# Fewer, longer VectorE instructions in a cached-attention decode kernel, and one small weight load in six pieces

## The chip, the cores and the metric
One core of a Trainium2 chip. The metric is the device time of one execution of the whole program in microseconds (us). The engines are TensorE (PE, its weight loads PEld), VectorE (DVE), ScalarE (ACT), GpSimd (POOL) and SyncE (SP, which here only issues transfers); 16 DMA engines move the data.

## What is computed
Four attention layers follow each other on one token's vector x of 640 numbers. Layers 0 and 2 use the caches and weights A, layers 1 and 3 those of B, so each cache is read twice. Each layer has 32 heads of 192 numbers and a cache of 8192 positions.

```python
q = (x @ wq).reshape(B, Sq, H, Dh)...
scores = jnp.einsum("bhqd,bhkd->bhqk", q, k_cache) * (Dh ** -0.5)
p = _softmax(scores, axis=-1)
o = jnp.einsum("bhqk,bhkd->bhqd", p, v_cache)
return ... @ wo

x = x + _A_ref(_layernorm(x, axis=-1), A_k_cache, A_v_cache, A_wq, A_wo)
x = x + _B_ref(_layernorm(x, axis=-1), B_k_cache, B_v_cache, B_wq, B_wo)
x = x + _A_ref(_layernorm(x, axis=-1), A_k_cache, A_v_cache, A_wq, A_wo)
x = x + _B_ref(_layernorm(x, axis=-1), B_k_cache, B_v_cache, B_wq, B_wo)
```

All is bf16 in memory, with float32 sums.

## The kernel before
The work goes by pairs of heads, 16 pairs in a layer, in the order of `ORDER` (layer 3 runs nearly backward). A pair's K is 6.3 MB, and so is its V: partition p holds 128 positions of one of the two heads, 64 partitions a head. It comes in two units of 64 positions a partition. SBUF has eight slots of a unit each (`pool`); wq and wo rows go through the same slots. A Python planner writes out the order: `steps` is the order of the computation, `plan` that of the transfers. All transfers but x's are issued by SP, in the plan's order; each waits for the event that frees its slot (`freed`, lines 331 and 345 to 394), and `ahead` (line 404) issues what it can after each step. Whoever needs a tile waits for its landing (`need`, line 396).

For each pair and layer:

- `products` (lines 589 to 614), for each unit: VectorE multiplies K in its slot by the pair's q, in four chunks of 48 of the 192 numbers of a head (line 599, 128 partitions x 64 positions x 48). TensorE adds them up with an identity matrix: for each chunk six matmuls of 512 columns (eight numbers of 64 positions) into one PSUM bank S (line 612 the first, the rest through `matmul_held`, line 58). TensorE waits for each chunk. The last matmul frees K's unit.
- `softmax` (lines 616 to 639): VectorE sums S over the eight numbers left (line 621, once a unit) and takes maxima (lines 623, 630), TensorE brings the maximum to all partitions, ScalarE makes the exponentials p (line 636).
- `values` (lines 641 to 686): TensorE multiplies p by V as it landed. For pairs 0 to 14 a matmul takes eight positions and two heads at a time (line 678 and line 58, 16 rows of 512 columns in four column groups), so O (128 x 1536, three PSUM banks) has 8 blocks of 192 numbers, of which each row of a group needs one. Pair 15 takes two positions at a time (`k = 2`).
- `gather` (lines 688 to 723): VectorE takes from each row of O the block that belongs to it: eight instructions on 192 numbers, the first (line 696) a multiplication by a column of the constant `pick`, the others (line 697) a multiplication with an addition to `acc`. `pick` is 1 where the row's position in its group is the block's, else 0. TensorE adds the rows of a head (line 710) and ScalarE puts them into a row, scaled by the softmax's sum (line 721). TensorE's next `values` waits for the gather (`last["O"]`, line 659). Pair 15 has two blocks and so two instructions (`end`).

After each five pairs the row becomes columns (`columns`, line 577, L581 and L584) and is multiplied by wo rows (`project`, line 531; `project_row`, line 563, in layer 3). The rows of the last pair are small: 384 rows of wo as 128 partitions x 3840 bytes, 480 KB (`wol`, lines 350 to 355; in layer 3 two transfers, `wol` and `woe`). `wol` is issued when `columns` of the third block is done (line 317), after V of pair 15. In layers 0 and 1 the next transfer behind it is the next layer's wq, 128 partitions x 61440 bytes in one (line 383) for layers 0 and 1, parts (line 386) for layers 2 and 3.

Pairs 14 and 15 stand differently (lines 248 to 281): the products of 15 come before the values of 14, and the gather of 14 after the softmax of 15. In layers 1 and 3 warm-up matmuls fill TensorE's waits at the end (`busy`, line 425, called at steps `busy` and in `values` and `gather`), and the last unit of V and the end of the third wo block come in two transfers (`vq`, `wob`). In layer 2 the wq parts lie in slots, pair 0's K is still there from layer 0, and TensorE does the query's matmuls between the two units of pair 0.

Everything that an engine executes stands in one queue for that engine (`Queue`), in program order, with explicit waits on semaphores; a queue is blocked by its first wait.

Of the kernel before, what the change touches and what calls it, by code (L numbers as in the profile page):

```python
# [5 lines left out]
ALU = mybir.AluOpType  # L6
AX = mybir.AxisListType
# [61 lines left out]
def build(nc, A_x, A_k, A_v, A_wq, A_wo, B_x, B_k, B_v, B_wq, B_wo, out):  # L69
    _, H, SK, DH = A_k.shape  # L70
    D = A_x.shape[-1]
    P = 128
# [3 lines left out]
    EPS = 1e-5  # L76
    NL = 4
    NPAIR = H // 2
    QD = DH // 4
    R = 512 // JU  # L80
    W = [dict(k=A_k, v=A_v, wq=A_wq, wo=A_wo), dict(k=B_k, v=B_v, wq=B_wq, wo=B_wo)]
    PD = 2 * DH
# [6 lines left out]
    OI = PD // P  # L89
    NB = [0, 5, 0, 7]  # L90
    G = 4
    VK = 8
    FORWARD = dict(pairs=list(range(NPAIR)), q0=0, q1=1, wo=[0, PAIRS_W, 2 * PAIRS_W], wol=NPAIR - 1)
    BACKWARD = dict(pairs=[15, 14, 11, 12, 13] + list(range(1, 11)) + [0], q0=NPAIR - 1, q1=0,
                    wo=[NPAIR - PAIRS_W, 1, 1 + PAIRS_W], wol=0)
    ORDER = [FORWARD, FORWARD, FORWARD, BACKWARD]

    with ExitStack() as ctx:
# [13 lines left out]
        rows = sb("rows", [P, QR], BF16)  # L112
# [3 lines left out]
        acc = sb("acc", [P, DH], F32)  # L116
# [10 lines left out]
        pick = col(VK)  # L127
# [25 lines left out]
        O = OY[:, 0:VK * DH]  # L153
# [5 lines left out]
        QMu, Ou, TBu, YBu = [(use[b],) for b in ("QM", "O", "TB", "YB")]  # L159
# [8 lines left out]
        DV = Queue(sem("pDVE"))  # L168
        AC = Queue(sem("pACT"))
        PO = Queue(sem("pPOOL"))  # L170
        SP = Queue()
# [3 lines left out]
        e = PO.op(lambda g: g.memset(ident[:], 0.0))  # L175
# [6 lines left out]
        e = PO.op(lambda g: g.memset(mask, 0.0))  # L182
# [162 lines left out]
        def transfer(n):  # L345
            l = n[1]
            o = ORDER[l]
            w = W[l % 2]
            free = [freed[b] for b in before[n]]
            if n[0] in ("wol", "woe"):  # L350
                r0 = o["wol"] * PD
                a, b = (0, OI) if l < 3 else (0, OI - 1) if n[0] == "wol" else (OI - 1, OI)
                return SP.op(lambda s: s.dma_start(
                    rows[:, a * D:b * D], w["wo"][r0:r0 + PD].rearrange("(p i) n -> p (i n)", p=P)[:, a * D:b * D]),
                    *free, sem=semOL if n[0] == "wol" else semOE, inc=16)
            if n[0] == "t":
                return max(free, key=lambda e: e[1]) if free else None
            if n[0] == "wob":
                r0 = o["wo"][2] * PD
                return SP.op(lambda s: s.dma_start(  # L360
                    slot[place[("wo", l, 2)]][:, (NW - NB[l]) * D:NW * D],
                    w["wo"][r0:r0 + PAIRS_W * PD].rearrange("(p i) n -> p (i n)", p=P)[:, (NW - NB[l]) * D:]),
                    sem=semOB, inc=16)
            if n[0] == "vq":
                n = ("v", l, NPAIR - 1, 1)
            i = place[n]
            t = slot[i]
            if n[0] in "kv":
                h = 2 * pair(l, n[2])
                r = w[n[0]][0, h:h + 2].rearrange("h (p j) d -> (h p) (j d)", j=J)  # L370
                if quarters(n):
                    x = TS // 2
                    if n in landed:
                        return SP.op(lambda s: s.dma_start(t[:, x:], r[:, TS + x:]), sem=semVQ, inc=16)
                    return SP.op(lambda s: s.dma_start(t[:, 0:x], r[:, TS:TS + x]), *free, sem=semS[i], inc=16)
                if whole(*n[:3]):
                    if n[3] == 1:
                        return landed[n[:3] + (0,)]
                    f = lambda s: s.dma_start(pool[:, i * TS:(i + 2) * TS], r)
                else:  # L380
                    f = lambda s: s.dma_start(t, r[:, n[3] * TS:(n[3] + 1) * TS])
            elif n[0] == "wq" and l < 2:
                f = lambda s: s.dma_start(pool[:, i * TS:i * TS + DC * QW], w["wq"].rearrange("(p c) n -> p (c n)", c=DC))
            elif n[0] == "wq":
                c0, k = Q_PARTS[n[2]]
                f = lambda s: s.dma_start(
                    wq_rows(l, n[2]),
                    w["wq"][:, o["q1"] * PD:o["q1"] * PD + QC].rearrange("(p c) n -> p c n", c=DC)[:, c0:c0 + k, :])
            else:
                r0 = o["wo"][n[2]] * PD  # L390
                k = NW - NB[l] if n[2] == 2 else NW
                f = lambda s: s.dma_start(
                    t[:, 0:k * D], w["wo"][r0:r0 + PAIRS_W * PD].rearrange("(p i) n -> p (i n)", p=P)[:, 0:k * D])
            return SP.op(f, *free, sem=semS[i], inc=16)
# [53 lines left out]
        def layer(l, ev_z, ev_true):  # L448
# [140 lines left out]
            def products(p, u):  # L589
                nk = ("k",) + first_load("k", l, p) + (u,)  # L590
                nt = ("t", l, p, u) if stays("k", l, p) else nk
                kin = slot[place[nk]].rearrange("p (j d) -> p j d", d=DH)
                k3 = slot[place[nt]].rearrange("p (j d) -> p j d", d=DH)
                qi = (l * NPAIR + p) % 2
                DV.wait(need(nk), need(nt), ev_q[p])
                chunks = []
                for c in range(4):
                    d0 = c * QD
                    e = DV.op(lambda v, d0=d0: v.tensor_tensor(  # L599
                        k3[:, :, d0:d0 + QD], kin[:, :, d0:d0 + QD],  # L600
                        q_sb[qi][:, d0:d0 + QD].unsqueeze(1).broadcast_to([P, JU, QD]), ALU.mult))
                    chunks.append(e)
                last["q"][qi] = chunks[-1]
                S = SP_[u]
                PE.wait(last["S"][u], ev_const)
                for c in range(4):
                    PE.wait(chunks[c])
                    for r in range(QD // R):
                        d0 = c * QD + r * R
                        fin = c == 3 and r == QD // R - 1  # L610
                        e = PE.op(lambda t, d0=d0, fin=fin: (
                            t.matmul(S[:, :], lhsT=ident[:], rhs=k3[:, :, d0:d0 + R], start=True, stop=fin) if d0 == 0 else  # L612
                            matmul_held(t, S[:, :], ident[:], k3[:, :, d0:d0 + R], False, fin)), signal=fin, bank=Su[u])
                freed[nt] = ev_S[p, u] = e
# [73 lines left out]
            def gather(p):  # L688

                end = p == NPAIR - 1  # L690
                a, n = (slice(0, P), 1) if end else (slice(96, 97), 2)
                ev_rl = last["rl"] = DV.op(lambda v: v.reciprocal(rl[a, 0:n], TB[a, C_L:C_L + n]), ev_l[p], last["TO"], bank=TBu)  # L692
                DV.wait(ev_O[p], last["acc"], ev_pick)
                for i in range(2 if end else VK):
                    e = DV.op(lambda v, i=i: (
                        v.tensor_scalar(acc[:], O[:, 0:DH], pick[:, 0:1], None, ALU.mult) if i == 0 else  # L696
                        v.scalar_tensor_tensor(out=acc[:], in0=O[:, i * DH:(i + 1) * DH], scalar=pick[:, i:i + 1], in1=acc[:],  # L697
                                               op0=ALU.mult, op1=ALU.add)), e if i else None, bank=Ou)
                last["O"] = e
                if end and l == 3:  # L700
                    busy(3)
                PE.wait(e, last["TO"], last["TT"])
                for h in range(2):
                    if end:
                        for c in range(OI):
                            e = PE.op(lambda t, c=c, h=h: t.matmul(
                                TB[64 * h:64 * h + 64, c:c + 1], lhsT=acc[:, c:DH:OI], rhs=half[:, h:h + 1],
                                start=True, stop=True), signal=(h == 1 and c == OI - 1), bank=TBu)
                    else:
                        e = PE.op(lambda t, h=h: t.matmul(  # L710
                            TB[96:97, C_O + h * DH:C_O + (h + 1) * DH], lhsT=half[:, h:h + 1], rhs=acc[:],
                            start=True, stop=True), signal=h == 1, bank=TBu)
                last["acc"] = e
                if end:
                    last["TTn"] = last["TO"] = AC.op(
                        lambda a: a.activation(oTl[:], TB[:, 0:OI], ACT.Copy, scale=rl[:, 0:1]), e, ev_rl, last["oTl"], bank=TBu)
                else:
                    o0 = (pair(l, p) - ORDER[l]["wo"][p // PAIRS_W]) * PD
                    AC.wait(e, ev_rl, last["orow"])
                    for h in range(2):  # L720
                        last["TO"] = last["row_written"] = AC.op(lambda a, h=h: a.activation(  # L721
                            orow[:, o0 + h * DH:o0 + (h + 1) * DH], TB[96:97, C_O + h * DH:C_O + (h + 1) * DH], ACT.Copy,
                            scale=rl[96:97, h:h + 1]), bank=TBu)
# [108 lines left out]
```

## Time and profile before

| what | value |
|---|---|
| time, median of 3 runs | 1981.71 us (1981.65 to 1982.63) |
| span of the profiled execution | 1982.1 us |
| HBM read | 848.36 MB, 428 GB/s over the span |
| slots' share of the traffic | all but 0.9 MB of 849.25 MB, by SP's queue |
| last V landed, last output issued | 1975.4, 1980.1 us |

The page divides the span into 40 slices and gives the granted TensorE clock in tenths of full speed, the busy share of the DMA engines and the rate:

```profile
PEclk9787776778677777777887877878787888777779
DMA  9999999999999999999999999999999999999998
```

The chain that ended last, followed back from the end:

```profile
DMA 67%; DVE 17%; PE 15%; ACT 1%; issue 0%; SPq 0%
```

Two thirds of it are transfers. VectorE's share in the chain is mostly line 599 where the chain goes from a landing through the products and S to the slot that is freed and the next transfer into it. A group's line on the page gives busy time and the mean of one in ns, then the idle time of the engine just before those instructions and what ended most of it. A line of the timeline has start and duration in us, engine, source line, operation, what is written and read, the count, and in brackets the idle time before.

### The profile page before, as it was taken

To read this page: it belongs to the slowest core of one execution; us is meant where nothing else is said; L and a number is where in the kernel's file an instruction comes from. 1 tells how busy PE (TensorE), PEld (TensorE's weight loads), DVE (VectorE), ACT (ScalarE), POOL (GpSimd) and SP (SyncE) were. 2 spreads that over 40 slices of the span, in tenths; PEclk is the share of its full clock that TensorE was granted. 3 is DMA by queue.
4 is the path that set the end of the run, shared out by engine and by line. 5 is a ranking of instruction groups with operands and counts; after the bars stand their busy time and mean duration, and the time that the engine had idled before them with its cause. 6 is when DMAs were issued, how large, how long until landed. Compare 5 with 4: busy or idle time off the path is not lost.

```text
span 1982.1 us, 13748 instructions
## 1 busy us (share of the span) xinstructions
PE 1288.6 (65%) x8248; PEld 146.4 (7%) x3160; DVE 1201.2 (61%) x1376; ACT 139.9 (7%) x462; POOL 4.5 (0%) x23
## 2 busy tenths in 40 slices
PE   3567476666466666666785676675776766657658
PEld 0001001000100100100020010010001001000001
DVE  3566467467166657556745565665764775665656
ACT  0000000000000000000010000000000100000000
POOL 0000000000000000000000000000000000000000
PEclk9787776778677777777887877878787888777779
DMA  9999999999999999999999999999999999999998
GB/s 414 438 431 430 431 436 432 430 430 429 435 432 433 434 430 432 429 435 433 426 407 426 425 426 426 432 430 431 434 429 427 435 431 433 433 432 431 433 433 367
DMA packets 26930, 849.25 MB, mean 428 GB/s; under 512 B 3058, under 2 KB 3188, under 8 KB 3828
## 3 DMA queue, kind: packets, MB, share of 16 engines
q1 hardware_dynamic: 26724, 848.38, 99.6%
q8 instruction: 45, 0.74, 0.2%
q14 instruction: 17, 0.14, 0.0%
q10 hardware_dynamic: 144, 0.00, 0.0%
HBM read 848.36 MB, written 0.00 MB: 428 GB/s over the span
## 4 chain that ended last, share of the span: by engine, by line
DMA 67%; DVE 17%; PE 15%; ACT 1%; issue 0%; SPq 0%
DMA pool<-in_B_k_cache_dram 27%; DMA pool<-in_A_v_cache_dram 20%; DVE pool L599 15%; DMA pool<-in_A_k_cache_dram 14%; PE S L58 6%; DMA pool<-in_B_v_cache_dram 6%; PE OY L58 5%; PE OY L678 3%; DVE acc L697 1%; ACT p_sb L636 1%; DVE s_sb L621 1%; PE S L612 0%; DVE m_bf L623 0%; PE OY L538 0%; PE QM L626 0%
## 5 line engine op out<-in xcount | busy, mean ns | idle before, releaser
L599 DVE TENSOR_TENSOR pool<-pool,q_sb 128x3072 bf16<-128x3072 bf16 x512 | 861.1, 1753 | 229.5 <-DMA pool<-in_B_k_cache_dram 133.5
L58 PE MATMUL S<-pool,ident 128*128 128x512 bf16 x2944 | 789.5, 425 | 19.5 <-DVE pool L599 17.6
L710 PE MATMUL TB<-acc,small 128*1 128x192 f32 x240 | 82.7, 495 | 212.0 <-DVE acc L697 212.0
L58 PE MATMUL OY<-pool,p_sb 128*16 128x512 bf16 x1920 | 202.7, 498 | 0.0
L696 DVE TENSOR_SCALAR acc<-OY,small 128x192 f32<-128x192 f32 x64 | 26.7, 418 | 287.5 <-PE OY L58 256.3
L678 PE MATMUL OY<-pool,p_sb 128*16 128x512 bf16 (+1 forms) x1216 | 148.2, 495 | 69.5 <-DMA pool<-in_A_v_cache_dram 63.5
L612 PE MATMUL S<-pool,ident 128*128 128x512 bf16 x128 | 61.8, 483 | 201.3 <-DVE pool L599 201.2
L697 DVE SCALAR_TENSOR_TENSOR acc<-OY,small,acc 128x192 f32<-128x192 f32 x424 | 177.1, 418 | 14.9
L621 DVE TENSOR_REDUCE s_sb<-S 128x64 f32<-128x512 f32 x128 | 88.0, 688 | 69.7 <-PE S L58 69.7
L527 ACT ACTIVATE q_sb<-QM 128x192 bf16<-128x192 f32 x60 | 19.9, 331 | 944.0 <-PE QM L521 944.0
L721 ACT ACTIVATE rows<-TB,small 1x192 bf16<-1x192 f32 x120 | 43.2, 406 | 596.3 <-PE TB L710 596.3
L692 DVE RECIPROCAL small<-TB 1x2 f32<-1x2 f32 x64 | 11.2, 175 | 94.5 <-PE TB L651 75.3
L636 ACT ACTIVATE p_sb<-s_sb,small 64x128 bf16<-64x128 f32 x128 | 55.7, 435 | 161.2 <-DVE small L630 160.4
L612 PEld LDWEIGHTS S<-pool,ident 128*128 128x128 bf16 x128 | 12.9, 101 | 676.2 <-DVE pool L599 604.4
L651 PE MATMUL TB<-small,ones 128*1 128x2 f32 x120 | 11.4, 165 | 74.1 <-ACT p_sb L636 74.1
L678 PEld LDWEIGHTS OY<-pool,p_sb 128*16 128x16 bf16 (+1 forms) x1216 | 39.8, 107 | 217.3 <-issue 138.8
L626 PE MATMUL QM<-ident,m_bf 128*64 128x64 bf16 x128 | 14.0, 216 | 54.4 <-DVE m_bf L623 53.9
L710 PEld LDWEIGHTS TB<-acc,small 128*1 128x1 f32 x240 | 19.8, 101 | 310.8 <-DVE acc L697 284.0
L630 DVE TENSOR_REDUCE small<-QM 128x1 f32<-128x64 f32 x64 | 14.4, 225 | 35.2 <-PE QM L626 35.2
L521 PEld LDWEIGHTS QM<-rows,one_b 1*64 1x64 bf16 x120 | 6.2, 100 | 347.0 <-issue 341.1
L538 PE MATMUL OY<-oT,pool 128*128 128x1 bf16 x675 | 28.6, 178 | 1.9 <-ACT oT L584 1.9
L538 PEld LDWEIGHTS OY<-oT,pool 128*128 128x128 bf16 x675 | 27.8, 131 | 3.8 <-ACT oT L584 2.5
(74 smaller groups left out, 215.2 us busy)
## 6 DMA issues: line engine op xcount, KB each, us to landing
pool<-in_B_k_cache_dram SPq DMA_DIRECT2D x28, 6144.0 KB, 37.9
pool<-in_B_v_cache_dram SPq DMA_DIRECT2D x28, 6144.0 KB, 33.5
pool<-in_A_v_cache_dram SPq DMA_DIRECT2D x27, 6144.0 KB, 27.5
pool<-in_A_k_cache_dram SPq DMA_DIRECT2D x34, 3072.0 KB, 20.5
pool<-in_A_k_cache_dram SPq DMA_DIRECT2D x14, 6144.0 KB, 36.4
pool<-in_A_v_cache_dram SPq DMA_DIRECT2D x10, 3072.0 KB, 14.7
pool<-in_B_k_cache_dram SPq DMA_DIRECT2D x8, 3072.0 KB, 22.5
pool<-in_A_wo_dram SPq DMA_DIRECT2D x6, 2400.0 KB, 21.9
```

The costliest lines, as they stand in the source:

```text
L58: return t.add_instruction(mybir.InstMatmult(name=t.bass.get_next_instruction_name(), engine=mybir.EngineType.PE, ins=[t.lower_ap(rhs), t. ...
L527: lambda a: a.activation(q_sb[i][:], QM[:, 0:DH], ACT.Copy), e, last["q"][i], bank=QMu)
L538: e = PE.op(lambda t, i=i, c=c, f=y_first[0], fin=n[0] == "wol" and i == k - 1: t.matmul(YB[:, c:c + 1], lhsT=t3[:, i, c:D:DC], rhs=o[:, i ...
L599: e = DV.op(lambda v, d0=d0: v.tensor_tensor(k3[:, :, d0:d0 + QD], kin[:, :, d0:d0 + QD], q_sb[qi][:, d0:d0 + QD].unsqueeze(1).broadcast_t ...
L612: t.matmul(S[:, :], lhsT=ident[:], rhs=k3[:, :, d0:d0 + R], start=True, stop=fin) if d0 == 0 else
L621: lambda v, u=u: v.tensor_reduce(s[:, u * JU:(u + 1) * JU], SP_[u][:].rearrange("p (j r) -> p j r", r=R), AX.X, ALU.add), ev_S[p, u], last ...
L636: ev_p[p] = AC.op(lambda a, h=h, r=r: a.activation(p_sb[par][r, :, h], s[r, :], ACT.Exp, bias=negm[par][r, 0:1], accum_out=l_col[par][r, h ...
L678: t.matmul(o, lhsT=x, rhs=y, start=f, stop=fin) if c == 0 else
L696: v.tensor_scalar(acc[:], O[:, 0:DH], pick[:, 0:1], None, ALU.mult) if i == 0 else
L697: v.scalar_tensor_tensor(out=acc[:], in0=O[:, i * DH:(i + 1) * DH], scalar=pick[:, i:i + 1], in1=acc[:], op0=ALU.mult, op1=ALU.add)), e if ...
L710: e = PE.op(lambda t, h=h: t.matmul(TB[96:97, C_O + h * DH:C_O + (h + 1) * DH], lhsT=half[:, h:h + 1], rhs=acc[:], start=True, stop=True), ...
L721: last["TO"] = last["row_written"] = AC.op(lambda a, h=h: a.activation(orow[:, o0 + h * DH:o0 + (h + 1) * DH], TB[96:97, C_O + h * DH:C_O ...
```

## The change
`products` makes two chunks of 96 numbers (12 matmuls each) instead of four of 48 (6 matmuls), but for pair 0 of layer 2, which keeps four. `gather` takes all eight blocks at once for pairs 0 to 14: a multiplication of O by `pick`, spread over the 192 numbers, in place in PSUM (128 x 1536), and a sum over the eight blocks into `acc`, read with a step of 192 numbers. The second waits for the first. Pair 15 keeps its two instructions. In layer 0 the last pair's wo rows come in six transfers of 1, 2, 4, 8, 112 and 1 partitions with the same wait and semaphore; those of the other layers stay one.

```diff
-    QD = DH // 4
...
+                if l == 0:
+                    w3 = w["wo"][r0:r0 + PD].rearrange("(p i) n -> p (i n)", p=P)
+                    for x, y in ((0, 1), (1, 3), (3, 7), (7, 15), (15, 127), (127, 128)):
+                        e = SP.op(lambda s, x=x, y=y: s.dma_start(rows[x:y, 0:OI * D], w3[x:y]), *free, sem=semOL, inc=16)
+                    return e
...
-                for c in range(4):
+                NC = 4 if l == 2 and p == 0 else 2
+                QD = DH // NC
+                for c in range(NC):
...
-                for c in range(4):
+                for c in range(NC):
                     PE.wait(chunks[c])
                     for r in range(QD // R):
                         d0 = c * QD + r * R
-                        fin = c == 3 and r == QD // R - 1
+                        fin = c == NC - 1 and r == QD // R - 1
...
-                for i in range(2 if end else VK):
-                    e = DV.op(lambda v, i=i: (
-                        v.tensor_scalar(acc[:], O[:, 0:DH], pick[:, 0:1], None, ALU.mult) if i == 0 else
-                        v.scalar_tensor_tensor(out=acc[:], in0=O[:, i * DH:(i + 1) * DH], scalar=pick[:, i:i + 1], in1=acc[:],
-                                               op0=ALU.mult, op1=ALU.add)), e if i else None, bank=Ou)
+                if end:
+                    for i in range(2):
+                        e = DV.op(lambda v, i=i: (
+                            v.tensor_scalar(acc[:], O[:, 0:DH], pick[:, 0:1], None, ALU.mult) if i == 0 else
+                            v.scalar_tensor_tensor(out=acc[:], in0=O[:, i * DH:(i + 1) * DH], scalar=pick[:, i:i + 1], in1=acc[:],
+                                                   op0=ALU.mult, op1=ALU.add)), e if i else None, bank=Ou)
+                else:
+                    o3 = O.rearrange("p (i d) -> p i d", d=DH)
+                    e = DV.op(lambda v: v.tensor_tensor(o3, o3, pick[:, 0:VK].unsqueeze(2).broadcast_to([P, VK, DH]), ALU.mult),
+                              bank=Ou)
+                    e = DV.op(lambda v: v.tensor_reduce(acc[:], O.rearrange("p (i d) -> p d i", d=DH), AX.X, ALU.add), e, bank=Ou)
```

## The prediction
> **What bounds the kernel now.** I read the page from the top: the load of the DMA engines, then the queues, the costliest groups, the waits, and the timeline at the places where the waits end.
>
> ```profile
> span 1982.1 us, 13748 instructions
> ...
> PE 1288.6 (65%) x8248; PEld 146.4 (7%) x3160; DVE 1201.2 (61%) x1376; ACT 139.9 (7%) x462; POOL 4.5 (0%) x23
> ...
> GB/s 414 438 431 430 431 436 432 430 430 429 435 432 433 434 430 432 429 435 433 426 407 426 425 426 426 432 430 431 434 429 427 435 431 433 433 432 431 433 433 367
> ...
> q1 hardware_dynamic: 26724, 848.38, 99.6%
> q8 instruction: 45, 0.74, 0.2%
> q14 instruction: 17, 0.14, 0.0%
> ```
> The queue that carries the caches works for 99.6% of 16 engines' span, so the kernel is bound by its transfers. VectorE is busy for 61%: what the change takes off it shows only where transfers wait for it. Three dips in GB/s are such places: the start (414), the passage from layer 1 to layer 2 (407, about 990 to 1060) and the end (367). Packet by packet, the engines' idle time sums to a mean of 5.4 us an engine after about 1970, 1.2 in 1000 to 1020, 0.35 in 1050 to 1060, 0.3 in 1180 to 1190, and next to nothing elsewhere. This is all that could be won or enlarged.
>
> ```profile
> L599 DVE TENSOR_TENSOR pool<-pool,q_sb 128x3072 bf16<-128x3072 bf16 x512 | 861.1, 1753 | 229.5 <-DMA pool<-in_B_k_cache_dram 133.5
> ...
> L696 DVE TENSOR_SCALAR acc<-OY,small 128x192 f32<-128x192 f32 x64 | 26.7, 418 | 287.5 <-PE OY L58 256.3
> ...
> L697 DVE SCALAR_TENSOR_TENSOR acc<-OY,small,acc 128x192 f32<-128x192 f32 x424 | 177.1, 418 | 14.9
> L621 DVE TENSOR_REDUCE s_sb<-S 128x64 f32<-128x512 f32 x128 | 88.0, 688 | 69.7 <-PE S L58 69.7
> ...
> L630 DVE TENSOR_REDUCE small<-QM 128x1 f32<-128x64 f32 x64 | 14.4, 225 | 35.2 <-PE QM L626 35.2
> ```
> Per pair VectorE runs eight L599 products, the softmax reductions and the gather (L696 once, L697 seven times). It waits 229.5 us for K in all.
>
> ```profile
> DVE pool L599 <- DMA pool<-in_B_k_cache_dram: 133.5, 30, 13.4
> DVE pool L599 <- DMA pool<-in_A_k_cache_dram: 94.6, 27, 9.8
> ...
> PE OY L678 <- DMA pool<-in_A_v_cache_dram: 63.5, 21, 10.9
> ```
> These 57 waits for K have a mean of 4.0 us, the 21 for A's V 3.0 us. In the ordinary pairs of layers 0, 1 and 3 VectorE stands idle 3 to 5 us between the gather and the next K (1.8 to 2.1 where a wo block comes between); in layer 2 it starts at once and TensorE waits for V instead. That is the cover of a longer pair.
>
> **The change, part by part.**
>
> *Products.* Eight in a row take 13.45 us, 1.68 each at their pace, so 3072 elements cost about 1.60 and 0.08 fixed. An instruction of 6144 would then take 3.28; the other bound is twice the mean of 1753 ns, 3.51. The pace is the nearer row, since these also run back to back: four take 13.12 us, a gain of 0.33 (bounds +0.6 to -0.33). But TensorE gets its chunks later. After the last product it has six matmuls to do now (1.46 us) and twelve afterwards: 2.92 by that row, 2.73 by a free run of 23 in 5.23 us. So S of a unit is ready about 1.0 us later (0.9 to 1.1), and so are the release of K's slot and the softmax; with the dearer product 1.9. In an ordinary pair this lies under the 3 to 5 us of waiting for K or V; SP issues its next transfer then with 8 to 35 us of work in the queue. Layer 2's first pair keeps four chunks.
>
> *Gather.* From the reductions out of PSUM, (688-225)/(512-64) = 1.03 ns an element and 0.16 us fixed: 1536 elements take 1.75 us. An instruction with two inputs has 0.418-192*0.00103 = 0.22 us fixed: 1.81. With 0.03 between them 3.59 us, against 0.42+0.03+3.13 = 3.58 now: no change. No row shows a strided read over three banks or an instruction that writes the PSUM it reads. Bounds: 0.86 ns an element, as the start's memset of 2048 elements in 1.76 us, gives 2.7 us, a gain of 0.9; 418/192 = 2.18 ns an element gives 3.34 each and 6.7 us, a loss of 3.1. I take the reductions' row: same engine, memory and type.
>
> *Two pairs in a row without a wait for K.* Pairs 14 and 15 of each layer run so, since V of 14 comes after the products of 15. There the delay counts twice: 2.0 to 2.2 us. At the end of the kernel:
>
> ```profile
> 1944.36 13.43 DVE L599 TENSOR_TENSOR pool<-pool,q_sb 128x3072 bf16<-128x3072 bf16 x8
> ...
> 1957.85 1.46 PE L58 MATMUL S<-pool,ident 128*128 128x512 bf16 x6 [0.21 <-DVE pool L599]
> ...
> 1973.06 1.24 PE L58 MATMUL S<-ident 128*128 128x512 bf16 x5
> 1975.43 0.82 PE L678 MATMUL OY<-pool,p_sb 128*4 128x384 bf16 x16 [1.12 <-DMA pool<-in_B_v_cache_dram]
> ...
> 1978.12 1.11 PE L570 MATMUL OY<-pool,oT 128*1 128x320 bf16 x14
> ```
> The eight are the products of pair 15, the six are its last matmuls, the last five of line 58 end the warm-up run at 1974.30, and 1975.43 is where the last V has landed. TensorE does all this in order, so 2.0 us later the warm-up ends at 1976.3 to 1976.5, 0.9 to 1.1 us after the landing; the last V, the gather of two instructions (unchanged) and L706 follow without slack to the projection at 1978.12. **+0.9 us** (0.6 to 1.2; 2.7 with the dearer product).
>
> At the end of layer 1 the same 2.2 us reach V14 (992.6 becomes 994.8) and the gather. TensorE waited there for V15's landings (to 1002.23, then to 1009.58 with TensorE free at 1008.4), which take up part. Layer 2's wq, issued at 1006.42 to a nearly empty queue, goes out 0.6 to 1.7 us later. Engines that are ahead idle longer, those behind still have work: **+0.5 us** (0 to 1.7). Layers 0 and 2 end with 6 to 7 us in the queue when the next transfer is issued: 0.
>
> *Instruction fetches.* They use the same DMA engines. 45*16384 bytes over 8248+3160 TensorE instructions are 65 bytes each. VectorE goes from 1376 instructions to 764: 252 products fewer (126 units lose two, two keep four) and 360 in the gathers (60 pairs lose six). At 65 bytes, 8 KB a fetch, that is 11 fetches and then 6. The trace has 16 landings for each transfer, one an engine; their spread grows from 1.06 us (first transfer) to 6.37 (landing at 985 to 991), falls after 1005, and reaches 6.10 for the last V. One engine is thrown back by 0.97 us at each of six fetches about 180 us apart (86, 267, 425, 620, 801, 981), about 6.1 pairs, which is VectorE's stream; it is the last at 991. With three instead of six it is not, but the next ones stand at 5.6 to 5.9, thrown back by about 1.5 us at a time by TensorE's 16 KB fetches, which stay. So **-0.5 us** at that landing, less where the pair's delay ends last: I take -0.3 (0 to -1.2). At the end the last engine is one that TensorE's fetch at 1963 threw back: 0.
>
> *wo rows.* One issue becomes six.
>
> ```profile
> 498.63 0.33 SPq L353 DMA_DIRECT2D rows<-in_A_wo_dram  x1
> ...
> 499.00 0.43 SPq L383 DMA_DIRECT2D pool<-in_B_wq_dram  x1
> ```
> Issues follow each other by 0.37 us, so five more take 1.9 us on SP (3.2 by the longest issue, 0.63). Behind them stands layer 1's wq alone, then K. With 2.0 of the pairs' delay wq goes out at 502.9. The engines run dry of V15 and these rows at 503.4 to 508.4 and the first transfer of the program took 1.0 us from issue to first packet: the earliest may idle about 0.5 us, the last, which sets wq's landing at 526.57, not at all. Without that cover it would be 1.9. A row of 3840 bytes takes 0.149 us. If few-partition pieces go to few engines, one engine may get 12 rows for 8 (+0.6) and others 7 (-0.15): 0 (bounds -0.15 to +0.6, none once engines have idled near 1005). The layer's rows landed at 508.42, 1.2 us behind the last V, and the layer waits for wq until 526.6.
>
> [...]
>
> Sum: 0.9+0.5-0.3 = +1.1 us. The profiled execution has 1982.1 as its span, 0.4 over the median of the runs, so the sum goes on the median: 1981.71+1.1 = **1982.8 us**.
>
> **The rivals.**
> 1. *The gather is dear.* If the multiply in PSUM costs 3.34 us, the gather grows by 1.5. An ordinary pair then needs 1.0+1.5 = 2.5 of its 3 us or more; the ends of layer 1 and 3 pay 1.5 each: 1982.8+3.1 = 1985.9, slower. It decides from 1.5 us on; from 2.0 the ordinary pairs pay as well, and at 3.1 some 58 of them pay about 1 us: over 2030. For: no such row. Against: the reductions' rate. Chance 0.19, the latter part 0.03.
> 2. *The thrown-back engine sets both halves.* If engine lag, not the pairs' chain, ends last at 1009 and 1978, three fetches fewer before and two after give up to -1.2 and -1: 1979.5. For: the spread of 6 us. Against: the next engines stand 0.5 us behind it. Chance 0.13.
> 3. *It does nothing:* the delay is swallowed at both ends by warm-up and landings: 1981.5. Chance 0.2.
>
> **How the numbers follow.** Forecast 0.48, rivals 0.19, 0.13, 0.2. The range reaches from rival 2 less 0.5 to rival 1 and the forecast's dear bounds: 1979.0 to 1988.0. 0.2%, about what a measurement can tell from no change, is 4.0 us: below 1977.7 only if more than half of all idle time went: 0.06. Above 1985.7: most of rival 1 and the forecast with several dear bounds: 0.22. Between: 0.72.
>
> **What would show it.** Products at 3.28 us, twelve matmuls after the last; a gather of 3.6 us; VectorE's wait for K smaller by about 1 us a pair; about 5 fetches fewer in the second instruction queue; TensorE without its wait for the last V. Wrong if VectorE no longer waits for K, if the multiply takes over 3 us, or if the engines idle before layer 1's wq.

## The result, and the profile after

The changed kernel takes **1987.12 us** (median of 17 runs, 1984.45 to 1990.57); the kernel before, beside it, 1982.22 (17 runs, 1981.65 to 1983.62). The ratio is 1.0023, with a 95% interval of 1.0016 to 1.0030: 4.9 us slower, just beyond the bound of 0.2% and 4.3 us above the forecast of 1982.8.

From the page of the changed kernel, the lines that answer to those of before (loads, rate in 40 slices, queues, costliest groups; in the new line numbers L605 are the products, L708 and L710 the gather, L627 the sums over S):

```profile
span 1985.5 us, 13141 instructions
...
PE 1270.5 (64%) x8248; PEld 145.4 (7%) x3160; DVE 1195.0 (60%) x764; ACT 139.8 (7%) x462; POOL 4.5 (0%) x23
...
GB/s 412 426 437 429 428 436 431 432 430 429 413 429 438 431 429 432 430 436 432 426 410 428 431 426 426 432 429 432 431 429 428 434 433 434 431 432 432 432 432 359
...
q8 instruction: 44, 0.72, 0.1%
q14 instruction: 13, 0.11, 0.0%
...
L605 DVE TENSOR_TENSOR pool<-pool,q_sb 128x6144 bf16<-128x6144 bf16 (+1 forms) x260 | 843.9, 3304 | 195.6 <-DMA pool<-in_B_k_cache_dram 110.8
...
L708 DVE TENSOR_TENSOR OY<-OY,small 128x1536 f32<-128x1536 f32 x60 | 106.0, 1767 | 229.6 <-PE OY L58 229.5
L627 DVE TENSOR_REDUCE s_sb<-S 128x64 f32<-128x512 f32 x128 | 88.2, 689 | 159.7 <-PE S L58 159.7
...
L710 DVE TENSOR_REDUCE acc<-OY 128x192 f32<-128x1536 f32 x60 | 105.5, 1758 | 2.0
```

VectorE has lost 44% of its instructions, and 6.2 us of its 1201.2 us of work: what is halved in number is doubled in length. Its wait for K shrinks from 229.5 to 195.6 us (0.5 us a pair), and its wait for S grows from 69.7 to 159.7 (1.4 us a pair). In the rate the eleventh slice, 495 to 545 us, has fallen from 435 to 413 GB/s: a dip at the end of layer 0, where the prediction costed six row pieces at nothing. The last slice has fallen from 367 to 359.

The packets tell it more finely. The trace has the start, duration and size of each packet. Two sums are taken from it, each shared out over the 16 engines: the idle time, which is the span less the time of all packets, and the slow time, which is what the packets of the cache queue take beyond the duration that nine in ten of their size reach or exceed. Slow time is 11.13 us an engine before and 13.65 after, 2.5 more; idle time is 4.44 and 5.46, 1.0 more. Together that is 3.5, against spans that differ by 3.4. At the end of layer 0 there are 2.3 us of slow packets (500 to 520 us) and 0.4 of idle time (500 to 510), where before there were under 0.15 and none; after 1970 there is 0.9 more idle time. Elsewhere losses and gains cancel. So the two places are the end of layer 0 and the end of the kernel. (The two profiled executions differ by less than the medians; why is in the last point of the section on the steps.)

### The profile page after: what moved, and what is told of

It is laid out like the page before. It is cut to its first block, busy times and chain, and to the rows that moved or that the text cites. A ratio compares the mean times of both kernels' runs of the same rounds, so it can differ in the third digit from the quotient of the medians.

```text
span 1985.5 us, 13141 instructions
## 1 busy us (share of the span) xinstructions
PE 1270.5 (64%) x8248; PEld 145.4 (7%) x3160; DVE 1195.0 (60%) x764; ACT 139.8 (7%) x462; POOL 4.5 (0%) x23
## 4 chain that ended last, share of the span: by engine, by line
DMA 58%; PE 25%; DVE 15%; ACT 1%; issue 1%; SPq 0%
DMA pool<-in_B_k_cache_dram 24%; DMA pool<-in_A_v_cache_dram 16%; PE S L58 15%; DMA pool<-in_A_k_cache_dram 15%; DVE pool L605 11%; PE OY L58 5%; PE OY L684 3%; DMA pool<-in_B_v_cache_dram 3%; ACT p_sb L642 1%; PE S L618 1%; DVE OY L708 1%; DVE s_sb L627 1%; DVE acc L710 1%; DMA pool<-in_A_wq_dram 1%; DVE m_bf L629 0%
## 5 line engine op out<-in xcount | busy, mean ns | idle before, releaser
L605 DVE TENSOR_TENSOR pool<-pool,q_sb 128x6144 bf16<-128x6144 bf16 (+1 forms) x260 | 843.9, 3304 | 195.6 <-DMA pool<-in_B_k_cache_dram 110.8
L708 DVE TENSOR_TENSOR OY<-OY,small 128x1536 f32<-128x1536 f32 x60 | 106.0, 1767 | 229.6 <-PE OY L58 229.5
L58 PE MATMUL OY<-pool,p_sb 128*16 128x512 bf16 x1920 | 192.7, 478 | 0.0
L627 DVE TENSOR_REDUCE s_sb<-S 128x64 f32<-128x512 f32 x128 | 88.2, 689 | 159.7 <-PE S L58 159.7
L684 PE MATMUL OY<-pool,p_sb 128*16 128x512 bf16 (+1 forms) x1216 | 142.2, 478 | 47.4 <-DMA pool<-in_A_v_cache_dram 42.8
L710 DVE TENSOR_REDUCE acc<-OY 128x192 f32<-128x1536 f32 x60 | 105.5, 1758 | 2.0
```

The source lines that it names most:

```text
L58: return t.add_instruction(mybir.InstMatmult(name=t.bass.get_next_instruction_name(), engine=mybir.EngineType.PE, ins=[t.lower_ap(rhs), t. ...
L605: e = DV.op(lambda v, d0=d0: v.tensor_tensor(k3[:, :, d0:d0 + QD], kin[:, :, d0:d0 + QD], q_sb[qi][:, d0:d0 + QD].unsqueeze(1).broadcast_t ...
L627: lambda v, u=u: v.tensor_reduce(s[:, u * JU:(u + 1) * JU], SP_[u][:].rearrange("p (j r) -> p j r", r=R), AX.X, ALU.add), ev_S[p, u], last ...
L684: t.matmul(o, lhsT=x, rhs=y, start=f, stop=fin) if c == 0 else
L708: e = DV.op(lambda v: v.tensor_tensor(o3, o3, pick[:, 0:VK].unsqueeze(2).broadcast_to([P, VK, DH]), ALU.mult), bank=Ou)
L710: e = DV.op(lambda v: v.tensor_reduce(acc[:], O.rearrange("p (i d) -> p d i", d=DH), AX.X, ALU.add), e, bank=Ou)
```

## The experiments

Each is the kernel before with the edit shown, unless said otherwise, timed beside the kernel before. Of each edit the lines that matter are shown; `...` stands for lines left out. Three theories were set against each other first: **A**, the later S at the ends of layers; **B**, the row pieces themselves; **C**, the gather in PSUM.

| run | us (runs, lowest to highest) | ratio to before, 95% |
|---|---|---|
| products alone | 1984.33 (11, 1982.93 to 1989.95) | 1.0012 (1.0003 to 1.0021) |
| gather alone | 1982.23 (11, 1981.39 to 1983.69) | 0.9996 (0.9987 to 1.0005) |
| six pieces alone | 1985.66 (11, 1984.87 to 1986.48) | 1.0016 (1.0007 to 1.0024) |
| products and gather | 1985.14 (11, 1983.61 to 1989.10) | 1.0014 (1.0005 to 1.0022) |
| six column pieces | 1982.43 (11, 1981.88 to 1983.52) | 1.0000 (0.9991 to 1.0009) |
| 16 + 112 partitions | 1985.38 (11, 1984.76 to 1986.28) | 1.0014 (1.0005 to 1.0023) |
| even, odd partitions | 1982.27 (11, 1981.87 to 1983.31) | 1.0000 (0.9991 to 1.0009) |
| lower, upper half | 1985.70 (11, 1985.06 to 1987.25) | 1.0017 (1.0008 to 1.0026) |
| four products at all ends | 1983.02 (11, 1982.08 to 1984.71) | 1.0003 (0.9995 to 1.0012) |
| four at the last end | 1983.22 (11, 1981.56 to 1984.70) | 1.0005 (0.9996 to 1.0014) |
| the change, both mended | 1983.97 (11, 1981.83 to 1986.01) | 1.0006 (0.9997 to 1.0015) |

The kernel before had a median of 1982.33 to 1982.43 beside them.

### Part by part

Products alone:

```
-                for c in range(4):
+                NC = 4 if l == 2 and p == 0 else 2
+                QD = DH // NC
+                for c in range(NC):
...
```

> The kernel before with the two-chunk products alone. Three theories on the +4.9 us of the whole change (1982.2 to 1987.1). A, the products: S of a unit is ready 1.0 us later (more at TensorE's half clock), doubled at each layer's end, so transfers are issued late where the queue is thin; A gives 1985 to 1987 here and the wider spread of times. B, the row pieces: they push layer 1's wq back by 1.9 us of issues into a queue that has run dry, and the engines restart slowly; B gives 1983 here, the end of the kernel alone. C, the gather in PSUM costs where it is on the path; C gives about 1982.5 here.

Gather alone:

```
...
+                else:
+                    o3 = O.rearrange("p (i d) -> p i d", d=DH)
+                    e = DV.op(lambda v: v.tensor_tensor(o3, o3, pick[:, 0:VK].unsqueeze(2).broadcast_to([P, VK, DH]), ALU.mult),
+                              bank=Ou)
+                    e = DV.op(lambda v: v.tensor_reduce(acc[:], O.rearrange("p (i d) -> p d i", d=DH), AX.X, ALU.add), e, bank=Ou)
```

> The kernel before with the two-instruction gather alone. Its profile measured 1.77 and 1.76 us against 3.58 for the eight, so A and B give no change or a little less for three fetches fewer: 1981.5 to 1982.3. C gives 1985 or more.

Six pieces alone:

```
+                if l == 0:
...
+                    for x, y in ((0, 1), (1, 3), (3, 7), (7, 15), (15, 127), (127, 128)):
+                        e = SP.op(lambda s, x=x, y=y: s.dma_start(rows[x:y, 0:OI * D], w3[x:y]), *free, sem=semOL, inc=16)
```

> The kernel before with layer 0's last wo rows in six pieces alone. A and C: wq is issued 1.9 us later, but the queue still has 5 us of work, so the engines do not idle: 1982.2 within 0.5. B: the pieces cost by themselves: 1984 or more, with idle engines between 500 and 515 us.

Products and gather together, the rows in one transfer:

> The changed kernel with layer 0's last wo rows in one transfer again, so products and gather alone. A: 1985 to 1987, near the changed kernel. B: 1983, what is left is the end of the kernel. If both only act together (the products' delay uses up the queue that would hide the pieces) this is 1984 and each part alone is within 1.5 us of before.

C falls for the gather by itself, which moves the time by less than 0.13% either way. A and B both hold in part. The pieces alone cost 3.3 us, more than products and gather together (2.7), and they alone make the dip: the run without them has 432 GB/s in that slice, the run of them alone 409. Products alone cost 1.9 us, and scatter the runs over 7 us, where the kernel before scattered over 3.0 in 33 runs.

### Why six pieces cost 3 us

The issues take a little less than the prediction said: from the first piece to wq there are 1.93 us instead of 0.37, so five more take 1.56 and not 1.9. From the timeline of the changed kernel, SP's queue at the end of layer 0 (columns: start, duration, instruction, count; in the kernel before the two stood at 498.63 and 499.00):

```profile
503.09 1.89 SPq L355 DMA_DIRECT2D rows<-in_A_wo_dram  x6
505.02 0.36 SPq L387 DMA_DIRECT2D pool<-in_B_wq_dram  x1
```

In the run of the six pieces alone they were issued at 498.75, 0.1 us from where the one transfer stood, with pair 15's V (V15) in the queue, and wq at 500.68. No engine idled. But from 503 to 510 us, while the rows were in flight, a packet of 24576 bytes of V15 took 1345 to 1596 ns in the mean of a microsecond (0.91 us in the same run just before), and one of 61440 bytes of wq about 3750 ns (2267 elsewhere). Nothing was late; everything in flight was slow. Two readings: the number of transfers (B2), or which partitions they go to (B1). Two runs part them. Six transfers of all 128 partitions, cut by columns:

```
...
+                    for x in range(0, OI * D, OI * D // 6):
+                        e = SP.op(lambda s, x=x: s.dma_start(rows[:, x:x + OI * D // 6], w3[:, x:x + OI * D // 6]), *free, sem=semOL, inc=16)
```

> The kernel before, with layer 0's last wo rows in six transfers that each cover all 128 partitions and 320 of the columns (640 bytes a packet). Six issues as in the change, but every transfer has its partitions spread as the one transfer had. Theory B1 (pieces whose partitions do not line up with those of the other transfers make everything in flight slow): the 24576-byte packets of V15 stay at about 0.91 us, and the time is that of before, 1982.4 (1982 to 1983; the smaller packets may cost some tenths). Theory B2 (six issues instead of one are what costs): about +3 us as in the run of the six pieces alone, 1985.5.

And two transfers, cut by partitions:

```
...
+                    for x, y in ((0, 16), (16, 128)):
+                        e = SP.op(lambda s, x=x, y=y: s.dma_start(rows[x:y, 0:OI * D], w3[x:y]), *free, sem=semOL, inc=16)
```

> The kernel before, with layer 0's last wo rows in two transfers, partitions 0 to 15 and 16 to 127. One issue more than before. Theory B1 (partitions that do not line up): most of the rows still go out of line, packets in flight slow to about 1.5 us for 24576 bytes, +2 to +3 us: 1984.5 to 1985.5. Theory B2 (number of issues): one fifth of the six pieces' cost, +0.6 us or less: 1983.0 at most.

Six cost nothing, two cost 3.0 us: the count of transfers isn't it. The second also shows that the pieces of 1 to 8 partitions aren't needed for it. It is left open whether any transfer of fewer than 128 partitions does harm (B3). So two transfers of 64 partitions each, once the even and the odd ones, once (the second line) the lower and the upper half, equal in all but the partitions, and with them the rows of wo, that make up each:

```
...
+                    for x in (slice(0, P, 2), slice(1, P, 2)):
+                    for x in (slice(0, P // 2), slice(P // 2, P)):
+                        e = SP.op(lambda s, x=x: s.dma_start(rows[x, 0:OI * D], w3[x]), *free, sem=semOL, inc=16)
```

> The kernel before, with layer 0's last wo rows in two transfers of 64 partitions each: the even ones, then the odd ones. [...] Theory B1 (partitions out of line with those of the other transfers): packets in flight keep about 0.91 us for 24576 bytes, time of before, 1982.4 (1982 to 1983). Rival B3 (any transfer of fewer than 128 partitions slows what is in flight): +2 to +3 us, as the two pieces of 16 and 112.

> [...] Theory B1: slow packets again, +1.5 to +3 us: 1984 to 1985.4. Rival B3: the same time as the even and odd ones.

Nothing against 3.4 us. The stretch from 500 to 515 us asked of each trace gives busy times, then the granted TensorE clock, the busy share of the DMA engines and the rate. The kernel before, the column pieces, the even and odd ones:

```profile
500.00:515.00 15.00, 10.55 (x168) 6.68 (x168) 2.07 (x12) 0.27 (x1) 0.21 (x1) 0.61 1.04 445
```
```profile
500.00:515.00 15.00, 11.26 (x172) 7.39 (x172) 1.89 (x11) 0.27 (x1) 0.00 (x0) 0.50 1.04 436
```
```profile
500.00:515.00 15.00, 11.22 (x172) 7.27 (x172) 1.47 (x9) 0.27 (x1) 0.00 (x0) 0.50 1.02 438
```

The pieces of 16 and 112, the halves, and the changed kernel:

```profile
500.00:515.00 15.00, 10.28 (x168) 6.48 (x168) 1.00 (x3) 0.45 (x2) 0.00 (x0) 0.57 1.05 363
```
```profile
500.00:515.00 15.00, 9.89 (x158) 6.14 (x159) 1.00 (x3) 0.27 (x1) 0.00 (x0) 0.50 1.07 370
```
```profile
500.00:515.00 15.00, 11.28 (x164) 6.60 (x162) 1.00 (x3) 0.90 (x3) 0.00 (x0) 0.50 1.02 371
```

The share is 1.02 to 1.07 in all six (a packet counts whole where it starts), the rate is 436 to 445 in the first three and 363 to 371 in the others. That is how a slow transfer differs from an absent one: the engines are as busy and move a sixth less. Against the even and odd ones the halves lose (438 - 370) * 15 us = 1.02 MB, 2.4 us at 428 GB/s; by the packets the slow time at 500 to 520 us is 3.1 us an engine in the halves, in the 16 + 112 and in the six pieces alone, and at most 0.2 in the column, even and odd pieces. So the cost depends on how the partitions are divided among the transfers, and it falls on the neighbours in the queue as well. In all these runs a partition gets the same row of wo, so a division of the partitions is also one of the places in HBM that are read; no run parts the two.

Why those, no trace shows, since it doesn't record which engine wrote which partition. The even and odd pieces were chosen on a guess of the author's about how a transfer's partitions are shared out among the engines, and theory B1's forecasts for them and for the halves rest on it; no run shows it. What "out of line" means is shown by the outcome alone: 1982.27 us for the even and odd ones, 1985.70 for the halves. In the run of 16 + 112, which of its two transfers costs the 3.0 us was not tried.

### Where the products cost

Four products kept for pairs 14 and 15, of every layer and of the last layer alone:

```
-                NC = 4 if l == 2 and p == 0 else 2
+                NC = 4 if l == 2 and p == 0 or p >= NPAIR - 2 else 2
```
```
+                NC = 4 if l == 2 and p == 0 or l == 3 and p >= NPAIR - 2 else 2
```

> The products in two instead of four as in the run of the products alone, but pairs 14 and 15 of every layer keep four. Theory A (the later S of a unit costs only where two pairs run without a wait for K, at the layers' ends): the time is that of before, 1982.4 to 1983. Rival A2 (the cost of some 2 us is spread over the ordinary pairs or comes with a lower granted clock): it stays at about 1984.3, with the same wide spread.

> The products in two instead of four, but pairs 14 and 15 of the last layer alone keep four: it parts the end of the kernel from the ends of layers 0 to 2. By the prediction's terms (+0.9 at the end, +0.5 at the end of layer 1) it gives back about 0.9 of the 1.9 us: 1983.4. If the end of the kernel is all of it: 1982.4. If the ends of layers 0 to 2 or the ordinary pairs are all of it: 1984.3.

Of the 1.9 us the last end gives back 1.1 by the medians and the other three ends 0.2; 0.6 stays. Each difference alone is within the intervals, but in order and size they are theory A's, and the scatter falls from 7 us to 2.6 and 3.1. By the medians the ends of layers 0 to 2 and the ordinary pairs cost little, and the end of the kernel is the place.

There the two products do more than the prediction said. TensorE's first matmul for pair 15 of the last layer in the kernel before (in brackets, idle time before), then the pair in the changed kernel's timeline:

```profile
1946.17 0.39 PE L612 MATMUL S<-pool,ident 128*128 128x512 bf16 x1 [1.99 <-DVE pool L599]
```

```profile
1947.11 13.15 DVE L605 TENSOR_TENSOR pool<-pool,q_sb 128x6144 bf16<-128x6144 bf16 x4
...
1950.51 0.61 PE L618 MATMUL S<-pool,ident 128*128 128x512 bf16 x1 [3.59 <-DVE pool L605]
1950.91 7.84 PE L58 MATMUL S<-pool,ident 128*128 128x512 bf16 x23
...
1958.81 5.13 PE L58 MATMUL S<-pool,ident 128*128 128x512 bf16 x23
```

TensorE waits 3.59 us for its first chunk (1.99 before), and then 24 matmuls take 8.24 us, though its one wait between them, for the second product, could end at 1953.69 (half of 13.15 us after the start). The same stretch cut in pieces, granted clock in the third column from the right; the first line is the same stage in the kernel before:

```profile
1946.20:1949.20 3.00, 2.95 (x10) 0.06 (x1) 3.00 (x2) 0.00 (x0) 0.00 (x0) 0.69 1.02 442
```

```profile
1950.50:1953.50 3.00, 2.99 (x8) 0.10 (x1) 3.00 (x1) 0.00 (x0) 0.00 (x0) 0.50 0.97 412
1953.50:1957.00 3.50, 3.50 (x11) 0.00 (x0) 3.50 (x3) 0.00 (x0) 0.00 (x0) 0.59 0.91 392
1957.00:1959.00 2.00, 2.00 (x11) 0.10 (x1) 2.00 (x1) 0.00 (x0) 0.00 (x0) 1.00 0.93 394
```

At half clock (0.50) 8 matmuls fill 3 us, and at full clock (1.00) 11 fill 2. From the start of the products to the last S the pair takes 16.76 us here (1947.11 to 1963.87) and 15.90 with the products alone (1944.09 to 1959.99), where the clock came back sooner (0.50 from 1947.40 to 1950.40, 0.84 to 1954.00). It takes 14.88 before and 14.87 with four products at the last end. So S is 1.0 us late as predicted in that run, and 1.9 in the changed kernel. Four chunks hide the lower clock better (0.69 over their first 3 us in both runs that keep them): TensorE then waits for VectorE's products anyway (0.21 us before each of the last two chunks). At the end of layer 0 the same costs 2.85 us: from the start of the products to the issue that the first unit frees it takes 11.72 us (475.87 to 487.59, mean clock 0.71) for 8.87 (473.94 to 482.81, 0.81).

When the clock falls, and after how long a wait, isn't shown: after the wait of 3.59 us it is 0.50 to 0.59 for 6.5 us, but after one of 1.99 too the mean clock is 0.69 over 3 us (the kernel before, as above, and four at the last end, 1944.6 to 1947.6). Whether the fall of the clock is also what scatters the runs isn't shown: the mean clock of a whole run doesn't follow its time (0.773 in the slowest run of the changed kernel, 0.772 in the fastest).

### Both causes mended

The changed kernel with column pieces and four products at all ends:

```
-                    for x, y in ((0, 1), (1, 3), (3, 7), (7, 15), (15, 127), (127, 128)):
+                    for x in range(0, OI * D, OI * D // 6):
...
-                NC = 4 if l == 2 and p == 0 else 2
+                NC = 4 if l == 2 and p == 0 or p >= NPAIR - 2 else 2
```

> The changed kernel with both causes taken out: layer 0's last wo rows in six transfers of all 128 partitions and 320 columns each, and four products for pairs 14 and 15 of every layer; the gather in two instructions and the halved products of the other pairs stay. If late S at the layers' ends and pieces out of line are the whole loss: the run of four products at the ends, 1983.0 (1982.2 to 1983.8), or within 0.8 us of the kernel before. If the gather and the halved products lose something together that neither loses alone: 1984.5 or more.

It gives back 3.2 of the 4.9 us; before lies within its interval. It stands 0.95 above the run without the gather's edit, between the two outcomes that were named, with a scatter of 4.2 us. Products and gather together likewise stand 0.8 above the products alone. Both differences are within the intervals; whether gather and products lose a little together stays open. No version beats the kernel before; the gather alone equals it.

## Why the prediction was right or wrong, step by step

- *Products at 3.28 us.* Right: four take 13.15 us, 3.29 each at their pace, and the mean of the group is 3304 ns with eight short ones in it. Against the 13.43 us of eight short ones before, that makes 1.61 us for 3072 elements and 0.07 fixed, where the step put 1.60 and 0.08 with no row to part them. The wait for K shrank by half of what was said, 0.5 us a pair for about 1.
- *S about 1.0 us later, hidden in the ordinary pairs.* Right in place: with four products at the ends only 0.6 us is left of the cost, with 0 in the interval. The size came as said in the run of the products alone; in the changed kernel, with TensorE at 0.50 to 0.59 for 6.5 us, it is 1.9, and 2.85 for a unit at the end of layer 0 (0.71 for 0.81). The pace of matmuls was read from rows at full clock (0.98 from 1056.29 to 1061.52 and 1.00 from 1957.85 to 1959.31 in the kernel before).
- *Gather 3.59 for 3.58.* Right: 1.767 and 1.758 us with 0.03 between them, 3.56. The row chosen, the reductions out of PSUM, was the right one: neither the strided read nor the write to PSUM costs more. Rival 1 falls with it.
- *End of the kernel +0.9.* Right: 1.1 by the runs, 0.9 by the engines' idle time after 1970, and TensorE no longer waits for the last V, as said. It came about in part otherwise, by the clock (0.50 to 0.59 for 6.5 us), so the size is in part luck.
- *End of layer 1 +0.5, layers 0 and 2 nothing.* Too small to part: 0.2 for the three together by the runs. One profile doesn't show it either: the idle time at 990 to 1065 us is 1.3 us an engine in that of the kernel before, 0.4 in that of the changed one, and none to 2.0 over all the runs.
- *Instruction fetches -0.3.* The second instruction queue went from 17 fetches to 13, four fewer for five, and the first from 45 to 44; no run shows a gain, though the gather alone (six instructions fewer a pair) lies 0.2 below, within its interval. Rival 2 (1979.5) and rival 3 (1981.5) are out: the time is above both.
- *"wo rows": 0 (bounds -0.15 to +0.6).* **This step failed.** "Without that cover it would be 1.9", said the step, and the cover was nearly there: the engines had V15 to move and idled for 0.4 us only. But it asked just when the pieces would start and on how many engines, never whether the transfers in flight beside them would keep their pace. They didn't; it cost 3.3 us in the run by itself. No row of the trace before could have given the price, since every large transfer there covers 128 partitions; the bounds should then have been wide, and were among the narrowest. The step's own sign of being wrong, idle engines before layer 1's wq, came too, but only as the 0.4 us in the changed kernel, and not in the run of the pieces alone. The number of transfers cost nothing: the six column pieces took 1982.43 us.
- *The sum.* +1.1 was +4.9. With the rows at 3.3 it would have been +4.4. The parts measured alone add up to more (3.3 + 2.7 = 6.0). In the changed kernel the pieces go out 4.3 us later than in the run of them alone, when less of V15 is in flight to be slowed: the slow time is 2.3 us for 3.1, and 0.4 of idle time comes back. V15's last unit was issued 4.8 us late (487.59 for 482.81): the products of pair 15 started 1.9 late, and the half clock with the later chunks made 2.85. So wq went out at 505.02, where the step had 502.9.
- *The base.* The step compared the span of before, 1982.1, with the median time of 1981.71. In the runs that show both, the time is 1.7 to 2.5 us above the span (median 1.83), so that execution was some 2 us slower than the median. The sum went on the median, so it does no harm, but it explains why the two spans differ by 3.4 and the medians by 4.9.

The range of 1979.0 to 1988.0 holds the time by luck: it reaches so far mainly for rival 1, and rival 1 wasn't the cause. "Slower by over 0.2%", which had 0.22, came true by a little, for a reason that none of the rivals named.

## What to carry to other kernels

In a kernel bound by its transfers, ask of every new transfer which partitions it writes, not only how many bytes and issues it has: here a transfer of 480 KB that was cut into ranges of partitions slowed all that was in flight (363 to 371 GB/s for 445), and the same bytes cut by columns, or into even and odd partitions, didn't (436 and 438). Longer instructions on an engine that wasn't the bound saved nothing (products alone 1984.33 us, gather alone 1982.23, for 1982.33 to 1982.43), and handed their results on later and in larger lumps; where two stages run without slack, above all at the kernel's end, that is paid (1.1 us at the last end here), so keep the fine cut there. A busy share near 1 doesn't say that transfers run at their pace (1.04 went with 445 GB/s here, and 1.05 with 363): set the rate beside it.

## What the runs showed of the hardware that was not expected

- Two transfers of 480 KB in all, to partitions 0 to 63 and 64 to 127, made packets of the transfers beside them take 1.4 to 1.5 us for 24576 bytes instead of 0.91, and about 3.65 for 61440 bytes instead of 2.27, for some 6 us. The same bytes to even and odd partitions left them at 0.92 and 2.28.
- Packets of 640 bytes, six to a row, cost the kernel nothing against 3840 in one: 32 ns each, 0.19 us a row for 0.15.
- After a wait of 3.59 us before a run of matmuls TensorE's granted clock was 0.50 to 0.59 for the next 6.5 us in the changed kernel's last pair, and 0.50 for 3 us in the run of the products alone. After one of 1.99 us in the kernel before it was 0.69 over 3 us.
- A multiplication over three PSUM banks onto itself takes 1.15 ns an element and a strided reduction of it 1.14, instruction overhead included.
